# Five of the last fourteen output stores issued from ScalarE's queue instead of SyncE's

## The chip, the core and the metric

The kernel runs on one core of a Trainium2 chip. The metric is the device time of one execution in microseconds (us); of several runs the median is taken. The engines are named as in the profile: PE (TensorE matmuls) and PEld (its weight loads), DVE (VectorE), ACT (ScalarE), POOL (GpSimd) and SP (SyncE). SPq and ACTq are the instruction queues of SP and ACT when they issue a DMA.

## The reference

Two sequence layers over 2048 positions and 640 channels are computed from separate inputs and put side by side in one output of 2048 rows and 1280 columns, in bf16.

```
# part A: a diagonal state-space layer (S5)
Bu = einsum("bld,pd->blp", x, B_bar)
for t in range(L): h = Lam_bar * h + Bu[:, t]          # complex, 640 states
y  = 2 * einsum("blp,dp->bld", hseq, Cmat).real + x * Dskip

# part B: shift filter, gate, long convolution, gate (H3)
kv = shift_filter(k) * v                                # 4 taps
y  = irfft(rfft(kv) * rfft(ssm_k)) + kv * ssm_D         # 4096-point transforms along the sequence
y  = q * y

out = concatenate([a, b], axis=-1)
```

## The kernel before, in words

Everything lives in one large SBUF tile, `arena`, and one PSUM tile, `acc`. Part A computes its recurrence as a tree of matmuls over blocks of 16 rows. Its last stage is `project` (L696 to L719), once for each of the 16 row residues: it loads 128 rows of x (L700), multiplies them by Dskip (L701, on DVE or POOL), runs 20 matmuls into PSUM (L711), adds the two on DVE (L715), and stores 128 rows of 640 columns (L719, 160 KB, rows of 1280 bytes). One residue, the last in time, is cut into two halves of 320 columns, each with its own L715 and L719 of 80 KB. The four x buffers are used in turn, so a load L700 must wait until the store that last read its buffer has landed.

Part B is a convolution by two-step transforms, done in two halves of 320 channels. Its last step, `r1` (L907 to L934), leaves PSUM through a DVE multiplication by q (L932), and `store` (L936 to L944) writes the result. Each call of `store` issues four DMAs of 32 partitions by 16 rows by 160 columns: 160 KB in 512 pieces of 320 bytes. There are 16 of these in all; the last eight, of the second half of the channels, become ready when L932 has run for the last time on their rows.

Nothing is scheduled at run time. Each step is recorded as an operation with a number; the table `ORDER` (L1055) lists all 796 in the order in which they are emitted, each with its engine letter (T for PE, V for DVE, A for ACT, G for POOL, S for SP) and a PSUM bank. So `790S0` is operation 790 on SP. Every engine runs its own list strictly in order: an instruction that waits holds up all that stand behind it on its engine. An operation that needs another's result waits on a semaphore of the engine that made it.

A DMA tells of its end through one of eight semaphores, DMAHW0 to DMAHW7. They are handed out in turn over all the DMAs of SP and ACT together, and a DMA is issued only when the one that held its semaphore before has landed completely. So no more than eight are under way, and a DMA of one queue may have to wait for one of the other.

The operations that matter here are, by number: the part B stores 565 to 568 and 571 and 574 (first half of the channels), 699 to 702 and 709 to 712 (second half); the part A stores 757, 795, 790, 777 and the two half stores 782 and 785; and 773, the last load of x, which feeds 774 (L701 on POOL) and with it the DVE addition 776 whose result 777 stores.

Of the kernel before, what the change touches and what calls it, by code (L numbers as in the profile page):

```python
# [20 lines left out]
PACT, PDVE, PPOOL, PPE, PSP = "A", "V", "G", "T", "S"  # L21
# [443 lines left out]
class PartA:  # L465
# [230 lines left out]
    def project(self, i):  # L696
        c, P, A = self.c, self.c.P, self.A
        rows = lambda t: t.rearrange("(s r) d -> r s d", r=16)[ROW0[i]]
        ys, src = c.v("YS", 640 * (i % 4), 640), rows(self.x2)
        P.add(f"ld_r{i}", {PSP: .5}, lambda e: e.dma_start(out=ys, in_=src), outs=[ys], nbytes=128 * 1280)  # L700
        P.add(f"xd{i}", {PDVE: dve(640, .52), PPOOL: 1.5}, lambda e: e.tensor_tensor(out=ys, in0=ys, in1=c.DR, op=ALU.mult), outs=[ys], ins=[ys, c.DR])  # L701
        lo = (2 if i == 0 else 1) if i < 2 else i % 2
        lh = [A[:, j, i // 2, lo:lo + 255:2] for j in range(10)]
        cuts = ((0, 1), (1, 2)) if i == 13 else ((0, 2),)
        for b0, b1 in cuts:
            g = P.group(b1 - b0)

            def mm(e, B, b0=b0, b1=b1):
                for b in range(b0, b1):
                    for j in range(10):  # L710
                        e.matmul(B[:, 512 * (b - b0):512 * (b - b0) + 320], lhsT=lh[j], rhs=self.CT[:, j, 320 * b:320 * b + 320],  # L711
                                 start=(j == 0), stop=(j == 9))
            ct, part = self.CT[:, :, 320 * b0:320 * b1], ys[:, 320 * b0:320 * b1]
            P.add(f"C{i}", {PPE: (b1 - b0) * 10 * .1355}, mm, ins=lh + [ct], group=g, nmm=10 * (b1 - b0))
            P.add(f"ev_C{i}", {PDVE: dve(320 * (b1 - b0))}, lambda e, B, part=part, n=b1 - b0: e.tensor_tensor(  # L715
                out=part.rearrange("p (b n) -> p b n", b=n), in0=B.rearrange("p (b n) -> p b n", b=n)[:, :, 0:320],
                in1=part.rearrange("p (b n) -> p b n", b=n), op=ALU.add), outs=[part], ins=[part], group=g)
            dst = rows(c.out)[:, 320 * b0:320 * b1]
            P.add(f"st_A{i}", {PSP: .5}, lambda e, dst=dst, part=part: e.dma_start(out=dst, in_=part), ins=[part], nbytes=128 * 640 * (b1 - b0))  # L719


class PartB:
# [213 lines left out]
    def store(self, hf, b0, nb):  # L936
        c, P = self.c, self.c.P
        Q = self.q[hf].rearrange("p (b x) -> p b x", x=160)
        for ce in range(4):
# [1 line left out]
            c0 = 640 + 320 * hf + 160 * el  # L941
            s = Q[32 * ce:32 * ce + 32, b0:b0 + nb, :]
            dst = c.out.rearrange("(a b) d -> a b d", b=64)[:, 32 * cc + b0:32 * cc + b0 + nb, c0:c0 + 160]
            P.add(f"st_B{hf}", {PSP: .2 + .02 * nb}, lambda e, s=s, dst=dst: e.dma_start(out=dst, in_=s), ins=[s], nbytes=32 * nb * 320)  # L944


KSETS = [(0, 1, 2), (3, 4, 5), (6, 7)]
# [88 lines left out]
def plain_order(P):  # L1036
# [17 lines left out]

ORDER = (  # L1055
# [39 lines left out]
)  # L1095


# [68 lines left out]
```

## Time and profile before

| what | value |
|---|---|
| median of 3 runs | 193.33 us (193.14 to 193.49) |
| span of the profiled execution, first to last instruction | 195.7 us |
| PE busy | 181.7 us, 93% |
| DVE, ACT, POOL busy | 165.3, 140.9, 78.1 us |
| queue q1 (SP's DMAs) | 103004 packets, 28.86 MB, 81.1% of 16 engines' span |

The profile shows one execution, and it is 2.4 us longer than the median of the runs without a profile; its own time is known only as its span of 195.7 us. Times below that come with a place ("at 185.08") count from the start of that span. In a timeline row stand the start, the length from there to the end of the last merged instruction, the engine, the line, the operation, what it writes and reads, the count, and in brackets the idle time before it. Rows of a DMA queue give the time for which the sequencer was occupied with issuing, not the transfer. The landing of a transfer is given from the start of its issue.

### The profile page before, as it was taken

How to read it: one execution, taken by the hardware profiler on the slowest of the kernel's cores; microseconds unless marked ns; L12 is line 12 of the kernel's file. 1: busy time of each engine (PE TensorE's matmuls, PEld its weight loads, DVE VectorE, ACT ScalarE, POOL GpSimd, SP SyncE). 2: the span in 40 equal slices, each digit the busy share in tenths (PEclk: the TensorE clock that was granted, in tenths of full speed). 3: DMA queues.
4: the chain of work that ended last, by engine and by line, in shares of the span. 5: the costliest groups of instructions: out<-in, count | busy, mean ns of one | idle time of the engine just before them, and what ended most of it. 6: DMA issues, size and time to landing. Idle time of an engine off the chain costs nothing.

```text
span 195.7 us, 7455 instructions
## 1 busy us (share of the span) xinstructions
PE 181.7 (93%) x3297; PEld 120.1 (61%) x3300; DVE 165.3 (84%) x228; ACT 140.9 (72%) x170; POOL 78.1 (40%) x62
## 2 busy tenths in 40 slices
PE   7699699999999999889998999999999999999980
PEld 2586334444455666565676675557678776977750
DVE  4686999337999898999999999999999999969840
ACT  2499936999999899999988999888747750750000
POOL 8979940530030000196805480876050209302020
PEclk9999979999999999999999999999999999999998
DMA  5999869989699999979993899511199970536985
GB/s 153 259 195 176 135 131 151 185 131 135 129 249 183 243 244 123 156 149 152 126 138 147 208 189 158 106 36 35 35 219 184 189 155 3 134 107 157 211 192 154
DMA packets 103786, 30.15 MB, mean 154 GB/s; under 512 B 97482, under 2 KB 103114, under 8 KB 103754
## 3 DMA queue, kind: packets, MB, share of 16 engines
q1 hardware_dynamic: 103004, 28.86, 81.1%
q10 hardware_dynamic: 750, 0.82, 1.4%
q8 instruction: 26, 0.43, 0.9%
q14 instruction: 6, 0.05, 0.1%
HBM read 12.30 MB, written 7.86 MB: 103 GB/s over the span
## 4 chain that ended last, share of the span: by engine, by line
PE 69%; ACT 10%; DMA 8%; DVE 5%; issue 4%; SPq 2%; ACTq 0%; DVEq 0%
PE acc L711 21%; PE acc L552 19%; PE acc L899 6%; PE acc L854 5%; DMA arena<-in_B_ssm_k_dram 4%; PE acc L571 4%; ACT arena L867 4%; PE acc L835 4%; PE acc L673 3%; PE acc L920 3%; DMA arena<-in_A_B_re_dram 2%; SPq L761 2%; PE acc L830 2%; ACT arena L498 2%; PE acc L672 1%
## 5 line engine op out<-in xcount | busy, mean ns | idle before, releaser
L552 PE MATMUL acc<-arena 128*128 128x512 bf16 (+1 forms) x220 | 47.8, 375 | 1.9 <-DVE arena L402 1.9
L711 PE MATMUL acc<-arena 128*128 128x320 bf16 x320 | 45.7, 299 | 0.0
L867 ACT CAST arena<-acc 128x960 bf16<-128x960 f32 (+1 forms) x40 | 35.2, 907 | 7.0 <-PE acc L854 6.4
L711 PEld LDWEIGHTS <-arena 128*128 128x128 bf16 x320 | 30.4, 98 | 12.6 <-ACT arena L867 0.4
L552 PEld LDWEIGHTS <-arena 128*128 128x128 bf16 x220 | 21.9, 102 | 23.7 <-DVE arena L402 2.2
L840 ACT CAST arena<-acc 128x1024 bf16<-128x1024 f32 x32 | 31.1, 1027 | 2.0 <-PE acc L835 1.5
L904 ACT CAST arena<-acc 128x1024 bf16<-128x1024 f32 x16 | 15.6, 1029 | 10.8 <-PE acc L899 10.8
L854 PE MATMUL acc<-arena 128*64 128x160 bf16 x512 | 22.2, 235 | 0.4 <-ACT arena L867 0.3
L701 POOL TENSOR_TENSOR arena<-arena 128x640 bf16<-128x640 bf16 x8 | 11.7, 1473 | 26.1 <-DMA arena<-in_A_x_dram 26.1
L854 PEld LDWEIGHTS <-arena 128*64 128x64 bf16 x512 | 17.9, 109 | 5.8 <-issue 1.7
L794 POOL TENSOR_TENSOR arena<-arena 128x2048 bf16<-128x2048 bf16 x2 | 8.5, 4246 | 28.3 <-DVE arena L198 28.3
L715 DVE TENSOR_TENSOR arena<-acc,arena 128x640 bf16<-128x640 f32 (+1 forms) x17 | 13.1, 782 | 6.3 <-PE acc L711 6.1
L883 POOL TENSOR_TENSOR arena<-arena 128x1280 bf16<-128x1280 bf16 x4 | 11.3, 2824 | 16.7 <-DVE arena L881 11.0
L794 DVE TENSOR_TENSOR arena<-arena 128x2048 bf16<-128x2048 bf16 x13 | 16.0, 1233 | 1.3 <-ACT arena L199 1.2
L840 DVE CAST arena<-acc 128x1024 bf16<-128x1024 f32 x8 | 9.7, 1221 | 6.8 <-PE acc L835 6.7
L673 PE MATMUL acc<-arena 128*128 128x512 bf16 (+2 forms) x50 | 12.8, 327 | 0.0
L835 PEld LDWEIGHTS <-arena 64*64 64x64 bf16 x960 | 9.3, 107 | 4.9 <-issue 1.3
L881 POOL TENSOR_TENSOR arena<-arena 128x1280 bf16<-128x1280 bf16 x3 | 7.8, 2617 | 11.0 <-ACT arena L867 6.1
L932 DVE TENSOR_TENSOR arena<-acc,arena 128x960 bf16<-128x960 f32 (+1 forms) x12 | 11.9, 1036 | 0.0
L878 DVE TENSOR_TENSOR arena<-arena 128x2560 bf16<-128x2560 bf16 x8 | 11.9, 1483 | 0.0
L835 PE MATMUL acc<-arena 64*64 64x64 bf16 x960 | 11.3, 194 | 0.4 <-ACT arena L840 0.2
L692 DVE TENSOR_TENSOR arena<-acc,arena 128x1024 bf16<-128x1024 f32 (+1 forms) x10 | 11.1, 1137 | 0.5 <-PE acc L673 0.5
(143 smaller groups left out, 309.9 us busy)
## 6 DMA issues: line engine op xcount, KB each, us to landing
out_dram<-arena SPq DMA_DIRECT2D x31, 160.0 KB, 3.2
arena<-in_B_ssm_k_dram SPq DMA_DIRECT2D x8, 320.0 KB, 4.8
kv_rows<-arena SPq DMA_DIRECT2D x5, 512.0 KB, 3.9
arena<-kv_rows SPq DMA_DIRECT2D x16, 160.0 KB, 4.4
arena<-in_A_x_dram SPq DMA_DIRECT2D x16, 160.0 KB, 3.4
arena<-in_B_q_dram SPq DMA_DIRECT2D x8, 320.0 KB, 5.5
arena<-in_A_B_re_dram ACTq DMA_DIRECT2D x3, 160.0 KB, 3.4
arena<-in_A_B_im_dram SPq DMA_DIRECT2D x3, 160.0 KB, 3.5
```

The costliest lines, as they stand in the source:

```text
L552: e.matmul(o, lhsT=self.BT[j][:, d, :], rhs=self.XP[:, d, lo:lo + n], start=(d == 0), stop=(d == 4), skip_group_check=True)
L673: e.matmul(B[:, o], lhsT=c.RR[:, n, j, :], rhs=fr(j, q, k), start=not by_pe, stop=True, skip_group_check=True)
L711: e.matmul(B[:, 512 * (b - b0):512 * (b - b0) + 320], lhsT=lh[j], rhs=self.CT[:, j, 320 * b:320 * b + 320], start=(j == 0), stop=(j == 9))
L715: P.add(f"ev_C{i}", {PDVE: dve(320 * (b1 - b0))}, lambda e, B, part=part, n=b1 - b0: e.tensor_tensor(out=part.rearrange("p (b n) -> p b n" ...
L794: P.add(f"ca{d}_{j}", tt, lambda e: e.tensor_tensor(out=t1, in0=t1, in1=t2, op=ALU.add), outs=[t1], ins=[t1, t2])
L835: e.matmul(B[64 * b:64 * b + 64, 512 * l + 64 * i:512 * l + 64 * i + 64], lhsT=lh[i][ps], rhs=F[ps, b, 64 * l:64 * l + 64], start=True, st ...
L840: P.add(f"e1{what}{hf}_{u}", {PACT: act(1024), PDVE: dve(1024)}, lambda e, B: c.CP[e](out=out, in_=(B.rearrange("p (l n s k) -> p k s l n" ...
L854: e.matmul(B[64 * s:64 * s + 64, 512 * b + 160 * i:512 * b + 160 * i + 160], lhsT=c.W[:, k, 64 * b:64 * b + 64], rhs=self.AS[hf][:, k, 160 ...
L867: c.CP[e](out=out, in_=b.rearrange("p r (k j n) -> p r k j n", k=n, j=4) if nj > 1 else b.rearrange("p r (k x) -> p r k x", k=n))
L878: P.add(f"pp{hf}", n1, lambda e: e.tensor_tensor(out=pt, in0=X, in1=Yk, op=ALU.mult), outs=[pt], ins=[X, Yk])
L904: P.add(f"er2{hf}_{u}", {PACT: act(1024), PDVE: dve(1024)}, lambda e, B: c.CP[e](out=out, in_=B.rearrange("p (s n b) -> p b s n", s=2, n=4 ...
L932: e.tensor_tensor(out=Q, in0=B.rearrange("p (g x) -> p g x", g=2)[:, :, 0:80 * n].rearrange("p g (x n) -> p g x n", n=40), in1=Q, op=ALU.mult)
```

## The change

Five operations get the letter A instead of S in `ORDER`: the part B stores 710, 700 and 699, the part A store 790, and the first of the two half stores, 782. The two calls that record stores allow ACT as an engine. No store changes its size, source or destination, and the list of operations has the same order.

```
-            P.add(f"st_A{i}", {PSP: .5}, lambda e, ...
+            P.add(f"st_A{i}", {PSP: .5, PACT: .5}, lambda e, ...
-            P.add(f"st_B{hf}", {PSP: .2 + .02 * nb}, lambda e, ...
+            P.add(f"st_B{hf}", {PSP: .2 + .02 * nb, PACT: .5}, lambda e, ...
 ORDER, its last rows:
-    574S0 696V6 711S0 779V0 795S0 698V0 788T6 710S0 701S0 774G0 700S0 709S0 780T0 783T1 789V6 776V2 790S0 702S0 699S0 777S0 781V0 784V1 782S0 785S0
+    574S0 696V6 711S0 779V0 795S0 698V0 788T6 710A0 701S0 774G0 700A0 709S0 780T0 783T1 789V6 776V2 790A0 702S0 699A0 777S0 781V0 784V1 782A0 785S0
```

On SP, from load 773 to the end of the program, the queue stood so before (the operations are 773, 574, 711, 795, 710, 701, 700, 709, 790, 702, 699 and 777; the two half stores 782 and 785, which follow, are left out):

```order
L700 DMA arena<-in_A_x_dram 128x640 [waits DMAHW7_49,DMAHW1_49]
L944 DMA out_dram<-arena 32x16x160 [waits DMAHW0_49]
L944 DMA out_dram<-arena 32x16x160
L719 DMA out_dram<-arena 128x640 [waits DMAHW2_49,DVE_49]
L944 DMA out_dram<-arena 32x16x160 [waits DMAHW3_49]
L944 DMA out_dram<-arena 32x16x160 [waits DMAHW4_49,DVE_49]
L944 DMA out_dram<-arena 32x16x160 [waits DMAHW5_49]
L944 DMA out_dram<-arena 32x16x160 [waits DMAHW6_49]
L719 DMA out_dram<-arena 128x640 [waits DMAHW7_49,DVE_49]
L944 DMA out_dram<-arena 32x16x160 [waits DMAHW0_49]
L944 DMA out_dram<-arena 32x16x160 [waits DMAHW1_49]
L719 DMA out_dram<-arena 128x640 [waits DMAHW2_49,DVE_49]
```

All these issues are SP's. The same stretch of SP with the change, from load 773 to the end of the queue (773, 574, 711, 795, 701, 709, 702, 777, 785):

```order
L700 DMA arena<-in_A_x_dram 128x640 [waits DMAHW3_49,DMAHW1_49]
L944 DMA out_dram<-arena 32x16x160 [waits DMAHW4_49]
L944 DMA out_dram<-arena 32x16x160 [waits DMAHW6_49]
L719 DMA out_dram<-arena 128x640 [waits DMAHW7_49,DVE_49]
L944 DMA out_dram<-arena 32x16x160 [waits DMAHW0_49,DVE_49]
L944 DMA out_dram<-arena 32x16x160 [waits DMAHW1_49]
L944 DMA out_dram<-arena 32x16x160 [waits DMAHW2_49]
L719 DMA out_dram<-arena 128x640 [waits DMAHW3_49,DVE_49]
L719 DMA out_dram<-arena 128x320 [waits DMAHW4_49,DVE_49]
```

Five issues have left SP, and the load and the nine stores that stay wait on other DMA semaphores than before. At the end of ACT's queue, behind its last cast L904, now stand 710, 700, 790, 699 and 782:

```order
L904 CAST arena<-acc 128x256x4 [waits DVE_49]
L944 DMA out_dram<-arena 32x16x160 [waits DMAHW3_49,DMAHW5_49,DMAHW0_49,DVE_49]
L944 DMA out_dram<-arena 32x16x160 [waits DMAHW7_49,DVE_49]
L719 DMA out_dram<-arena 128x640 [waits DMAHW1_49,DVE_49]
L944 DMA out_dram<-arena 32x16x160 [waits DMAHW6_49,DMAHW4_49,DMAHW2_49]
L719 DMA out_dram<-arena 128x320 [waits DMAHW5_49,DVE_49]
```

Before, nothing stood behind that cast. Which DMA held a semaphore before follows from the turn in which they are handed out; the framework places the five of ACT earlier in that turn than they stand in `ORDER`. This is the turn of the end of the program, read out of the two built programs:

| | DMAHW0 | 1 | 2 | 3 | 4 | 5 | 6 | 7 |
|---|---|---|---|---|---|---|---|---|
| before, first round | 571 | 757 | 567 | 566 | 568 | 565 | 712 | 773 |
| second | 574 | 711 | 795 | 710 | 701 | 700 | 709 | 790 |
| third | 702 | 699 | 777 | 782 | 785 | | | |
| changed, first round | 571 | 757 | 567 | 710 (ACT) | 566 | 568 | 565 | 700 (ACT) |
| second | 712 | 790 (ACT) | 699 (ACT) | 773 | 574 | 782 (ACT) | 711 | 795 |
| third | 701 | 709 | 702 | 777 | 785 | | | |

A DMA waits for the one above it in its column to land. So with the change 773 waits for 710, 795 for 700, 709 for 790, and 702 for 699: four issues of SP wait for the landing of a store that ACT issues.

More of the change, by code (lines that the diff above doesn't have):

```diff
@@ L718, in project @@
             dst = rows(c.out)[:, 320 * b0:320 * b1]
-            P.add(f"st_A{i}", {PSP: .5}, lambda e, dst=dst, part=part: e.dma_start(out=dst, in_=part), ins=[part], nbytes=128 * 640 * (b1 - b0))
+            P.add(f"st_A{i}", {PSP: .5, PACT: .5}, lambda e, dst=dst, part=part: e.dma_start(out=dst, in_=part), ins=[part], nbytes=128 * 640 * (b1 - b0))
 class PartB:
@@ L943, in store @@
             dst = c.out.rearrange("(a b) d -> a b d", b=64)[:, 32 * cc + b0:32 * cc + b0 + nb, c0:c0 + 160]
-            P.add(f"st_B{hf}", {PSP: .2 + .02 * nb}, lambda e, s=s, dst=dst: e.dma_start(out=dst, in_=s), ins=[s], nbytes=32 * nb * 320)
+            P.add(f"st_B{hf}", {PSP: .2 + .02 * nb, PACT: .5}, lambda e, s=s, dst=dst: e.dma_start(out=dst, in_=s), ins=[s], nbytes=32 * nb * 320)
 KSETS = [(0, 1, 2), (3, 4, 5), (6, 7)]
```

75 rows, old and new, of the table ORDER are left out of this document.

## The prediction

> **What bounds the kernel now.** I read the busy time by stretches of the last 16 us first, then the timeline there, then the chain of waits, then the landing times of stores. The columns of the stretches are: stretch, its length, busy time and count of PE, PEld, DVE, ACT and POOL, granted clock, busy share of the 16 DMA engines, GB/s.
>
> ```profile
> 180.00:183.50 3.50, 3.50 (x145) 2.68 (x144) 3.50 (x5) 0.00 (x0) 0.00 (x0) 1.00 0.99 220
> 183.50:184.00 0.50, 0.50 (x6) 0.36 (x4) 0.50 (x2) 0.00 (x0) 0.00 (x0) 1.00 0.20 42
> 184.50:187.50 3.00, 3.00 (x24) 2.17 (x23) 0.83 (x2) 0.00 (x0) 1.40 (x1) 1.00 0.97 237
> 187.50:188.00 0.50, 0.50 (x5) 0.35 (x4) 0.50 (x2) 0.00 (x0) 0.00 (x0) 1.00 0.43 99
> 188.00:193.50 5.50, 1.93 (x15) 1.18 (x12) 1.70 (x4) 0.00 (x0) 0.00 (x0) 1.00 0.93 220
> 179.70:193.50 13.80, 10.23 (x194) 7.31 (x191) 7.82 (x11) 0.00 (x0) 1.40 (x1) 1.00 0.90 210
> ```
>
> PE sets the pace until 190, at full clock; ACT does nothing here. The DMA engines are nearly full from 180 to 193.5, with two holes, and idle for 0.10 x 13.8 = 1.4 us in all. The timeline of the same stretch:
>
> ```profile
> 173.01 1.93 ACT L904 CAST arena<-acc 128x1024 bf16<-128x1024 f32 x2 [1.16 <-PE acc L899]
> 177.37 3.28 DVE L932 TENSOR_TENSOR arena<-acc,arena 128x960 bf16<-128x960 f32 x3
> 178.54 3.07 SPq L944 DMA_DIRECT2D out_dram<-arena  x5
> 181.71 1.63 SPq L700 DMA_DIRECT2D arena<-in_A_x_dram  x1
> 183.38 0.96 SPq L944 DMA_DIRECT2D out_dram<-arena  x2
> 184.26 0.81 DVE L932 TENSOR_TENSOR arena<-acc,arena 128x640 bf16<-128x640 f32 x1
> 184.44 0.51 SPq L719 DMA_DIRECT2D out_dram<-arena  x1
> 184.99 3.42 SPq L944 DMA_DIRECT2D out_dram<-arena  x4
> 185.85 1.40 POOL L701 TENSOR_TENSOR arena<-arena 128x640 bf16<-128x640 bf16 x1 [8.59 <-DMA arena<-in_A_x_dram]
> 187.25 1.95 DVE L715 TENSOR_TENSOR arena<-acc,arena 128x640 bf16<-128x640 f32 x3 [2.17 <-PE acc L711]
> 188.51 0.87 SPq L719 DMA_DIRECT2D out_dram<-arena  x1
> 189.42 1.36 SPq L944 DMA_DIRECT2D out_dram<-arena  x2
> 189.97 0.49 DVE L715 TENSOR_TENSOR arena<-acc,arena 128x320 bf16<-128x320 f32 x1 [0.76 <-PE acc L711]
> 190.88 1.91 SPq L719 DMA_DIRECT2D out_dram<-arena  x3
> ```
>
> From 178.5 on SP issues with hardly a pause, about 0.61 us apiece (5 in 3.07). The last addition on DVE ends at 189.97 + 0.49 = 190.46, but the store of its result, the last of three in the last row, is issued only at 192.2. It is 1.7 us late because the queue ahead of it is long. What follows on it:
>
> ```profile
> SPq L1161 <- DMA out_dram<-arena: 1.9, 2, 1.7
> L719 SPq DMA_DIRECT2D out_dram<-arena x1: 619/619/619, 192.2 to 192.2; - x1
> 189.97 0.49 DVE arena L715
> ```
>
> The first row (SP's own waits) says that SP, done with issuing at 190.88 + 1.91 = 192.79, waits 1.9 us more for stores: the last lands at 194.7, that is 2.5 us after its issue. Another 1.0 us of closing semaphores makes the span of 195.7. The last row is the last piece of the chain of waits: it ends with DVE at 190.46, since it doesn't follow SP's queue, so the final 5 us have to be read off SP and the DMAs. What can move the end is the moment at which operation 785, the last half store, is issued, and how long it takes to land.
>
> **The change part by part.** What is removed: five issues of about 0.6 us from SP's stretch between 181.7 and 192.8, some 3.0 us. On ACT they cost nothing to compute: its last cast ends at 173.01 + 1.93 = 174.94, so nothing is queued behind the five. The bytes and pieces of the transfers are the same. An issue from ACT costs about the same as from SP:
>
> ```profile
> 2.17 0.45 ACTq L488 DMA_DIRECT2D arena<-in_A_B_im_dram  x1
> ```
>
> What is added are waits of SP for landings of ACT's stores, by the turn of the eight DMA semaphores: 773 for 710, 795 for 700, 709 for 790, 702 for 699. Before, each of SP's DMAs in this stretch waited for one that SP had issued eight places earlier and that had landed already: the chain of waits and SP's waits name no such hold between the stores. Now the partner in each pair is ready late, since it itself waits for DVE. The price of such a wait is the time from issue to landing, minimum/median/maximum: first the part B stores issued at 178.5 to 181.0, then those from 185.0 to 190.2, then part A stores from 184.4 to the end, then the load 773, then the loads of the last 26 us, then all part A stores, and the one part B store at 165.8 that had little beside it.
>
> ```profile
> DMA to landing us min/median/max: 3.1/3.8/4.4
> DMA to landing us min/median/max: 3.2/3.6/4.4
> DMA to landing us min/median/max: 2.9/3.1/3.3
> DMA to landing us min/median/max: 4.0/4.0/4.0
> arena<-in_A_x_dram SPq DMA_DIRECT2D x3, 160.0 KB, 3.1
> DMA to landing us min/median/max: 1.8/2.8/6.2
> DMA to landing us min/median/max: 2.6/2.6/2.6
> ```
>
> Now in order of time.
>
> *710 and 773.* 710 needs the third L932 of its row, which ends at 177.37 + 3.28 = 180.65. ACT issues it then (before: 184.99), and it lands 3.8 us later, at 184.5. SP has sent 712 by 181.6 and stands before load 773 until 184.5; before, it issued it at 181.7. The load lands at 184.5 + 3.1 = 187.6 instead of 181.71 + 4.0 = 185.7. POOL's 1.40 us and about 0.1 us ahead of it follow: 189.1 instead of 187.25. Addition 776 waits for that and ends at 189.1 + 0.83 = 189.9 (DVE L715, 479 to 826 ns, the row below) instead of 188.8; the two half additions follow, 0.48 and 0.49, so the last ends at 190.9 instead of 190.46. Price at the end: nothing as long as 785 is issued after 190.9, which the next steps make sure of; 0.4 us if they don't.
>
> ```profile
> L715 DVE TENSOR_TENSOR arena<-acc,arena x4: 479/653/826, 187.3 to 190.0; 128x640 bf16<-128x640 f32 x2, 128x320 bf16<-128x320 f32 x2
> ```
>
> *700 and 795.* SP sends 574 and 711 from 184.5 to 185.7 and stands before 795. 700 needs the L932 that ends at 184.26 + 0.81 = 185.07; issued then from ACT, it lands 3.6 later, at 188.7. SP sends 795 at 188.7 (before 184.44) and 701 at 189.3, and is free at 189.9.
>
> *790 and 709, 699 and 702.* 790 needs the first L715 of its row, which ends at 187.25 + 0.83 = 188.08. ACT issues 790 at 188.1 and, 0.6 later, 699 at 188.7. The first lands 3.1 later, at 191.2, and lets SP send 709 until 191.8. The second lands 3.6 later, at 192.3, and only then can SP send 702. Behind it stand 777 at 192.9 and 785 at 193.5 (pitch 0.6). 785 lands 2.5 us later, as before: 196.0.
>
> Before, it landed at 194.7. **The sum** is 188.1 + 0.6 + 3.6 + 2 x 0.6 + 2.5 = 196.0, that is 1.3 us more. The closing 1.0 us stays. Against its own time the profiled execution goes from 195.7 to 197.0; I carry the same 1.3 us over to the median of the runs, which lies 2.4 us under that span: 193.3 + 1.3 = 194.6.
>
> Bounds of the sum: with the shortest rows (2.6 for 699, a pitch of 0.48 as in the two issues that took 0.96, 1.8 for 785) the end is 188.1 + 0.5 + 2.6 + 1.0 + 1.8 = 194.0, or 0.7 less than now. With the longest (4.4, a pitch of 0.87, 3.3) it is 188.1 + 0.9 + 4.4 + 1.7 + 3.3 = 198.4, or 3.7 more. I take the medians of the crowded stretch, because what is held back (795 and 701) goes out at 188.7 to 189.9, beside 790 and 699: the four compete for the same 16 engines.
>
> A rule of the Trainium skill speaks against any gain: "DMA: Bandwidth & Descriptors", section "Issuing engines are not separate DMA queues", says that DMAs of different issuers share the same 16 engines and interleave, so that spreading them saves only the sequencer's issue time. The trace agrees as far as it goes, with shares of 0.99, 0.97 and 0.93; by that rule alone the most to be saved is the lag of 1.7 us, of issue time, and the sum would end near nothing. The same page, section "Queues, rings and completion order", says that an increment of a DMA's semaphore lands only after every earlier write of that engine, across its queues; no row here shows that, and it would lengthen the landings on which SP waits, not shorten them.
>
> **The rivals.** *Faster: the relief of SP wins.* If the landings that SP waits for come soon, SP has no backlog and sends 785 as soon as DVE is done: at 190.5 to 190.9, and 2.5 later it has landed, at 193.0 to 193.4, a gain of 1.3 to 1.7. The engines' idle time of 1.4 us caps that; with one half of the holes filled it is 0.7. Time: 192.0 to 192.6. The point from which it decides: 785 must be sent before 192.2, so 702 before 191.0 and 699 must land within 2.3 us of 188.7. For it speaks that SP, not DVE, is late now, and that the DMA engines are emptier while SP stands still; against it, that no part B store in the trace landed in less than 2.6.
>
> *No change: the DMA engines are the bound.* The same bytes must go through engines that are 93% busy to the end. If 699 lands in 3.0, the pitch is 0.5 and 785 lands in 2.3, the end is 188.6 + 3.0 + 1.0 + 2.3 = 194.9: 0.2 us more, time 193.5. For it speaks that a store that is held back finds emptier engines later; against it, that the issue is held in turn, pair by pair, so that emptied engines stay empty.
>
> *Much slower.* A part B store of this stretch took 4.4 us to land. If 699 does that and the rest is as forecast, the end is 0.8 later still, 196.8, a loss of 2.1; time 195.4 and above. For it speak the four stores competing from 188 on; against it, that the 4.4 were seen earlier, with PE still running and more stores under way.
>
> *The five don't come early on ACT.* They would, if the queue of ACT held them up. It is empty of work from 174.94, so I give this nothing.
>
> **How the numbers follow.** A change below 0.2% (0.4 us) can't be told from none. The forecast, a loss of 0.4 to 2.1 us, has 0.54 and its own range of 193.8 to 195.4; much slower has 0.12, no change 0.16, faster 0.18. That makes 0.66 for slower, 0.16 for the same, 0.18 for faster. The predicted time is 194.6. The range that should hold 8 in 10 must take in no change and the edge of the faster case, and most of the heavy one: 192.9 to 195.8.
>
> **What would show it.** In the changed kernel's timeline SP's issue of L700 should stand near 184.5, with a gap of 2 to 3 us ahead of it; the L719 behind the next two L944 near 188.7, with another gap; POOL's L701 should end near 189; SP's last L719 should be issued near 193.5; and SP's waits should name DMA out_dram ahead of L944 and L719, which they don't now. DMA shares should show holes near 183 to 185 and 187 to 189. The prediction is wrong if SP's last L719 is issued before 192, or if L700 goes out at 181.7 as before, which would mean that the DMA semaphores aren't shared between the queues as I read them.

## The result, and the profile after

| | median | ratio to before | 95% interval |
|---|---|---|---|
| before | 193.24 us (192.97 to 193.49) | | |
| with the change | 195.75 us (194.93 to 198.71) | 1.0109 | 1.0070 to 1.0148 |
| the same pair in a later comparison (e7 below) | 195.61 us beside 193.51 | 1.0099 | 1.0064 to 1.0134 |

The change makes the kernel about 1% slower: by the two ratios 2.1 and 1.9 us, where 1.3 us were forecast. The ratio leaves out the longest of the four runs with the change, 198.71 us, and the profile below is of that run, so positions in it are compared with each other, and lengths from PE's last matmul on, not its span with that of before.

From the timeline of the changed kernel, the stretch that was shown of before (up to 180 everything lies 0.44 us earlier here than there):

```profile
176.21 4.01 DVE L932 TENSOR_TENSOR arena<-acc,arena 128x640 bf16<-128x640 f32 x4
180.24 4.78 ACTq L944 DMA_DIRECT2D out_dram<-arena  x2
181.17 8.33 PE L711 MATMUL acc<-arena 128*128 128x320 bf16 x60
185.02 0.36 SPq L700 DMA_DIRECT2D arena<-in_A_x_dram  x1
185.43 1.24 SPq L944 DMA_DIRECT2D out_dram<-arena  x2
187.48 0.74 SPq L719 DMA_DIRECT2D out_dram<-arena  x1
187.68 0.36 ACTq L719 DMA_DIRECT2D out_dram<-arena  x1
188.15 0.38 ACTq L944 DMA_DIRECT2D out_dram<-arena  x1
188.31 4.23 SPq L944 DMA_DIRECT2D out_dram<-arena  x3
189.36 1.39 POOL L701 TENSOR_TENSOR arena<-arena 128x640 bf16<-128x640 bf16 x1 [12.74 <-DMA arena<-in_A_x_dram]
190.79 1.62 DVE L715 TENSOR_TENSOR arena<-acc,arena 128x640 bf16<-128x640 f32 x3 [3.15 <-POOL arena L701]
192.04 0.36 ACTq L719 DMA_DIRECT2D out_dram<-arena  x1
192.64 1.05 SPq L719 DMA_DIRECT2D out_dram<-arena  x2
```

The load 773 (L700) goes out at 185.02, where before it went out at 181.71. Three stores of SP that need no DVE result of that time, 701, 709 and 702, take 4.23 us from the start of the first to the end of the third instead of 0.6 each. POOL's L701 starts at 189.36 instead of 185.85. SP's own waits in this stretch (what waited, for what, us in total, times, longest):

```profile
SPq L700 <- DMA out_dram<-arena: 4.1, 1, 4.1
SPq L944 <- DMA out_dram<-arena: 3.2, 2, 2.3
SPq L1160 <- DMA out_dram<-arena: 2.0, 2, 1.9
SPq L719 <- DMA out_dram<-arena: 0.7, 1, 0.7
```

The row of the closing line existed before (L1161 there). A row of L700 did too, with 1.4 us, but for the load before 773, which went out at 176.15; before, neither 773 nor any store behind it waited for a landing. Now the other three rows are the four new waits for landings: 773 4.1 us, 795 0.7, and the 3.2 us of L944 are 2.3 of 709 (for 790) and 0.9 of 702 (for 699). Together that is 8.0 us in which SP stands still. The chain of waits of the second profile (e7) names the first of them:

```profile
176.79 1.07 DVE arena L932
177.89 4.48 DMA out_dram<-arena
182.43 3.59 DMA arena<-in_A_x_dram
186.13 1.43 POOLq L1160
188.80 0.40 DVE arena L715
```

The L932 that ends at 177.86 releases a store of ACT, whose landing 4.48 us later releases SP's load, whose landing releases POOL (its piece is named by the instruction behind it), and then the last additions. Before, the end of this chain was plain matmul work and one addition. And the DMA engines, in stretches of the changed kernel, columns as before:

```profile
179.30:182.90 3.60, 3.60 (x146) 2.75 (x145) 3.60 (x5) 0.00 (x0) 0.00 (x0) 1.00 1.02 223
182.90:185.50 2.60, 2.60 (x21) 1.87 (x20) 1.75 (x3) 0.00 (x0) 0.00 (x0) 1.00 0.28 61
191.00:192.50 1.50, 0.00 (x0) 0.00 (x0) 1.41 (x3) 0.00 (x0) 0.00 (x0) 1.00 0.49 105
180.00:195.00 15.00, 9.50 (x188) 6.91 (x187) 7.09 (x11) 0.00 (x0) 1.39 (x1) 0.95 0.79 184
```

A share of 0.28 for 2.6 us while 773 is held, and 0.49 for 1.5 us at the end, for most of which 702 is held: holes that later work doesn't fill. From 180 to 195 the share is 0.79; before it was 0.90 from 179.7 to 193.5.

### The profile page after: what moved, and what is told of

Its sections match the earlier page's. It is cut to its first block, busy times and chain, and to the rows that moved or that the text cites. A ratio compares the mean times of both kernels' runs of the same rounds, so it can differ in the third digit from the quotient of the medians.

```text
span 196.8 us, 7460 instructions
## 1 busy us (share of the span) xinstructions
PE 180.6 (92%) x3297; PEld 118.8 (60%) x3300; DVE 165.5 (84%) x228; ACT 141.1 (72%) x170; POOL 78.1 (40%) x62
## 4 chain that ended last, share of the span: by engine, by line
PE 59%; DMA 15%; DVE 8%; issue 6%; SPq 4%; ACT 4%; POOLq 1%; DVEq 1%
PE acc L552 20%; PE acc L711 14%; PE acc L899 6%; DMA arena<-in_B_ssm_k_dram 4%; PE acc L571 4%; PE acc L854 4%; DMA arena<-in_A_B_im_dram 4%; PE acc L835 4%; DMA arena<-kv_rows 3%; PE acc L673 2%; DMA out_dram<-arena 2%; DMA arena<-in_A_x_dram 2%; DVE arena L932 2%; ACT arena L867 2%; SPq L761 2%
## 5 line engine op out<-in xcount | busy, mean ns | idle before, releaser
L711 PE MATMUL acc<-arena 128*128 128x320 bf16 x320 | 45.7, 299 | 0.0
L711 PEld LDWEIGHTS <-arena 128*128 128x128 bf16 x320 | 30.4, 98 | 12.6 <-ACT arena L867 0.4
L701 POOL TENSOR_TENSOR arena<-arena 128x640 bf16<-128x640 bf16 x8 | 11.7, 1475 | 29.7 <-DMA arena<-in_A_x_dram 29.7
L904 ACT CAST arena<-acc 128x1024 bf16<-128x1024 f32 x16 | 15.5, 1027 | 10.8 <-PE acc L899 10.8
L932 DVE TENSOR_TENSOR arena<-acc,arena 128x960 bf16<-128x960 f32 (+1 forms) x12 | 12.0, 1038 | 0.0
```

Of the source, the lines that this page charges most:

```text
L904: P.add(f"er2{hf}_{u}", {PACT: act(1024), PDVE: dve(1024)}, lambda e, B: c.CP[e](out=out, in_=B.rearrange("p (s n b) -> p b s n", s=2, n=4 ...
L932: e.tensor_tensor(out=Q, in0=B.rearrange("p (g x) -> p g x", g=2)[:, :, 0:80 * n].rearrange("p g (x n) -> p g x n", n=40), in1=Q, op=ALU.mult)
```

## The experiments

The theory: SP loses time because its issues wait for landings of ACT's stores, through the semaphores that the two queues share. The rivals: a store issued from ACT, or two queues at once, lands later in itself; or the DMA engines are full and everything else is a detail. All ratios are to the kernel before on the same chip, with 95% intervals. The tail is the length from the end of PE's last matmul to the end of the span in the kernel's profile: its last row of L711 and its span give it. It leaves out what happened earlier in that execution. In the first profile of before the row was

```profile
181.61 8.33 PE L711 MATMUL acc<-arena 128*128 128x320 bf16 x60
```

so PE ended at 189.94, and the tail was 195.7 - 189.94 = 5.8 us.

| run | on ACT | SP's issues held by ACT's stores | ratio | 95% interval | tail, us |
|---|---|---|---|---|---|
| before, e5 | none | none | 1.0004 | 0.9979 to 1.0028 | 5.8, 5.5 |
| the change, e7 | five | four | 1.0099 | 1.0064 to 1.0134 | 7.3, 7.1 |
| e1, e6 | the same five | none | 0.9985; 1.0005 | 0.9940 to 1.0030; 0.9976 to 1.0034 | 4.2, 4.5 |
| e2 | 782 | one | 1.0077 | 1.0046 to 1.0109 | 7.4 |
| e8 | 710 | one, 1.1 us, early | 1.0009 | 0.9974 to 1.0045 | 5.6 |
| e4 | four | three, not the load | 1.0102 | 1.0062 to 1.0142 | 7.1 |
| e3 | seven | none that delays it | 1.0000 | 0.9953 to 1.0046 | 4.9 |
| e9 | none, 3 extra loads | none | 1.0021 | 0.9987 to 1.0055 | 5.6 |
| e10 | the five of e1, 3 extra loads | none (785 1.0 us, by SP's own 702) | 0.9989 | 0.9949 to 1.0029 | 5.3 |

**e1: the same five stores, another turn of semaphores.** The framework interleaves the engines' lists by a model of time before it hands out the semaphores. An option makes it use another model:

```
-    with _tile.TileContext(nc) as tc:
+    with _tile.TileContext(nc, schedule_with_timeline_sim=True) as tc:
```

Every engine's list keeps its order; only the DMA semaphores of the end of the program differ. The kernel before comes out the same with and without it. The turn is now 571, 757, 567, 566, 568, 565, 710, 712, then 773, 574, 711, 795, 700, 701, 709, 702, then 790, 699, 777, 782, 785.

> The change itself, with every engine's list in the same order and the same five stores on ACT; only the turn in which the eight DMA semaphores are handed out is another (the framework interleaves the engines by another model of time). Now 773 waits for 571, 795 for 566, 709 for 710 and 702 for 712, 785 for 700: all of them landed early. Theory of the holds (SP waits for late landings of ACT's stores): no hold is left, SP's load 773 goes out near 181.7 again, the last store is issued within 0.6 us of DVE's end, and the time falls under that of before: 192.3 us (191.8 to 192.9). Rival of the two queues (issuing from ACT or interleaving two queues slows the landings themselves): the loss stays, 195.0 to 196.5 us. Rival of the full DMA engines: no change against before, 193.0 to 193.5.

From its timeline, and SP's waits in it:

```profile
180.87 0.88 SPq L700 DMA_DIRECT2D arena<-in_A_x_dram  x1
188.27 2.00 SPq L719 DMA_DIRECT2D out_dram<-arena  x2
189.41 0.49 DVE L715 TENSOR_TENSOR arena<-acc,arena 128x320 bf16<-128x320 f32 x1 [0.77 <-PE acc L711]
SPq L1160 <- DMA out_dram<-arena: 2.3, 2, 2.1
SPq L719 <- DVE arena L715: 1.9, 2, 1.2
SPq L944 <- DVE arena L932: 1.6, 2, 1.3
```

193.26 us, ratio 0.9985: the whole loss is gone with the waits, though the same five stores come from ACT's queue at the same places. No issue is held by a store's landing any more, SP waits for DVE instead, and its last store goes out with the end of the last addition. So ACT as an issuer costs nothing that the interval shows (0.3% at most, where the change loses 1%), and the rival of the two queues falls. The gain that the theory expected as well, about 1 us, is not there in the times.

**e2: one store on ACT, with one late wait.** Against before, one letter in the order table (with ACT allowed for stores, as in the change), which by the turn makes 702 wait for 782:

```
-782S0
+782A0
```

> One store alone on ACT, 782, the first half store; its place in the turn makes SP's 702 wait for its landing. Theory of the holds: 782 is issued at 189.2 after its DVE addition and lands near 192.1; SP stands before 702 until then, and 702, 699, 777 and 785 follow at 0.5 to 0.6 us, so the last landing is near 196.2 instead of 194.7 and the time is 194.8 us (194.2 to 195.6), although four of the five are back on SP. Rival of the two queues: with one store of 80 KB on ACT a fifth of the loss at most, 193.2 to 193.8. Rival of SP's relief: 192.7 to 193.2.

```profile
184.50 0.80 SPq L719 DMA_DIRECT2D out_dram<-arena  x1
185.63 0.35 ACTq L719 DMA_DIRECT2D out_dram<-arena  x1
188.39 0.85 SPq L944 DMA_DIRECT2D out_dram<-arena  x2
SPq L944 <- DMA out_dram<-arena: 3.1, 1, 3.1
```

195.35 us, ratio 1.0077. SP is done with 790 at 185.30 and sends 702 at 188.39, the moment that 782 has landed; from 186.3 to 188.4 the DMA engines stand at a share of 0.20. One late wait of 3.1 us costs three quarters of the change's loss, with four of the five stores back on SP.

**e8: one store on ACT, without a late wait.** Again one letter, of 710 instead; then 795 waits for it, which was expected to land about when SP gets there.

```
-710S0
+710A0
```

> One store alone on ACT as in e2_one_held, but 710 instead of 782: the one issue of SP that has to wait for it is 795, and 710 has landed near 184.5, when SP gets there anyway. Theory of the holds: no loss, ratio 0.996 to 1.002, against 1.008 for the other single store. Rival that any store on ACT costs: 1.004 to 1.010 as there.

```profile
SPq L719 <- DMA out_dram<-arena: 1.1, 1, 1.1
190.25 1.88 SPq L719 DMA_DIRECT2D out_dram<-arena  x3
```

Ratio 1.0009. The wait is 1.1 us, early in the stretch, and SP has caught up by its last row, so nothing is left of it at the end (the tail is 5.6 us). With e2 this says that it isn't the number of stores on ACT that counts, but which landing SP has to wait for.

**e4: the change without the late load.** Store 710 is on SP, the other four on ACT. 773 waits for 567; the new waits are 795 for 700, 701 for 790, 709 for 699 and 785 for 782.

```
-710A0
+710S0
```

> The change with store 710 back on SP: 773 then waits for 567 and goes out near 181.7, but 795 waits for 700, 701 for 790, 709 for 699 and 785 for 782. Theory of the holds, if the queue's chain of stores alone carries the loss: POOL's L701 ends near 187.3 and DVE near 190.5 as before, SP sends 701 when 790 has landed (near 191), 709 when 699 has (near 192.2), 785 near 194, and the time is 195.0 us (194.3 to 196.0). If the late load carries it: as before or faster, 192.5 to 193.5. Rival of the two queues: about four fifths of the loss, 194.5 to 195.5, but with SP's issues going out on time.

```profile
184.63 1.40 POOL L701 TENSOR_TENSOR arena<-arena 128x640 bf16<-128x640 bf16 x1 [8.45 <-DMA arena<-in_A_x_dram]
188.97 0.49 DVE L715 TENSOR_TENSOR arena<-acc,arena 128x320 bf16<-128x320 f32 x1 [0.76 <-PE acc L711]
191.81 1.28 SPq L719 DMA_DIRECT2D out_dram<-arena  x2
SPq L719 <- DMA out_dram<-arena: 4.0, 1, 4.0
SPq L944 <- DMA out_dram<-arena: 2.3, 3, 1.0
```

Ratio 1.0102, as with the change. Here POOL is on time and DVE ends 0.5 us after PE (180.61 + 8.32 = 188.93), so the load isn't needed for the loss: the queue of stores carries it alone, 6.3 us of SP's waiting in the last two rows. Of these, 4.0 are 795's and 1.0 is that of 709, while 785 was not held, and 1.0 is 711's wait for 565, a store of SP itself. The late load is real, but in the change it runs beside the other chain.

**e3: seven stores on ACT, no late wait of a store.** 574, 711, 795, 710, 709, 701 and 700 are on ACT. SP's waits are 773 for 566, 790 for 795, 777 for 701 and 785 for 700.

> Seven stores on ACT (574, 711, 795, 710, 709, 701, 700) and a turn in which no issue of SP waits for a late one: 773 waits for 566 and 757, 790 for 795, 777 for 701, 785 for 700. Theory of the holds: nobody is held, SP has only 773, 790, 702, 699, 777, 782 and 785 left; faster than before, 192.2 us (191.6 to 192.9). Rival of the two queues: more on ACT is worse than the change, 195 to 197 us. Rival of the full DMA engines: as before, 193.0 to 193.5.

```profile
181.25 5.94 ACTq L944 DMA_DIRECT2D out_dram<-arena  x4
183.20 1.06 SPq L700 DMA_DIRECT2D arena<-in_A_x_dram  x1
188.25 1.39 POOL L701 TENSOR_TENSOR arena<-arena 128x640 bf16<-128x640 bf16 x1 [12.02 <-DMA arena<-in_A_x_dram]
189.68 1.62 DVE L715 TENSOR_TENSOR arena<-acc,arena 128x640 bf16<-128x640 f32 x3 [2.24 <-POOL arena L701]
```

Ratio 1.0000, not the gain that was expected. The load went out at 183.20 and POOL could start only at 188.25: about 4.9 us for a load that took 4.0 before, now beside ACT's early stores. The last addition ended at 189.68 + 1.62 = 191.30 and the last store followed it at 191.45, so in this profile the later load set the end. The tail is shorter than before all the same, which the times don't show.

**e5, e6, e7: before, e1 and the change once more, with new profiles.** They were to say whether e1's shorter tail is real.

> The kernel before, unchanged: for a second profile of it, since the first one is a single execution. Expected of all theories: ratio 1.000; from PE's last matmul to the end of the span 5.8 us as in the first profile (5.3 to 6.3). If it is nearer 4.5, the lag of 1.7 us that SP showed in the first profile is not always there, and the relief of SP is worth less than 1.6 us.

> The change with the other turn of semaphores, as in e1_turn, once more and beside a second profile of the kernel before. Theory of the holds: no loss. What is open is the gain: its tail from PE's last matmul to the end was 4.2 us in the profile against 5.8 before, which would be worth 1.6 us (0.8%), while the times showed 0.15% with an interval of 0.45% to either side. If the tail decides, the ratio is 0.992 to 0.996; if the lag of the first profile was a chance, 0.997 to 1.001.

> The change, unchanged, for a second profile and a better interval. Theory of the holds: ratio 1.007 to 1.013; tail from PE's last matmul to the end 7.3 us (6.8 to 7.8); load 773 is issued the moment 710 has landed, 702 the moment 699 has, and DVE's last addition ends 2 to 3 us after PE's last matmul instead of 0.5.

The last issues of SP in e5, e6 and e7, in this order, each below PE's last row of the same profile:

```profile
179.20 8.32 PE L711 MATMUL acc<-arena 128*128 128x320 bf16 x60
187.91 2.12 SPq L719 DMA_DIRECT2D out_dram<-arena  x3
178.37 8.32 PE L711 MATMUL acc<-arena 128*128 128x320 bf16 x60
185.60 2.00 SPq L719 DMA_DIRECT2D out_dram<-arena  x2
178.82 8.32 PE L711 MATMUL acc<-arena 128*128 128x320 bf16 x60
190.09 1.04 SPq L719 DMA_DIRECT2D out_dram<-arena  x2
```

PE ends at 187.52, 186.69 and 187.14; SP is through with issuing 2.5, 0.9 and 4.0 us after that. The tails repeat the first profiles within 0.4 us. The times repeat too: 1.0099 for the change, 1.0005 for e1's turn. So the profile shows a tail that is 1.0 to 1.6 us shorter without the late waits than before, and the times, some twenty runs of that turn, show no gain. One of the two must have another part in it, and the next pair was made for that. The trace does give a ground for the shorter tail: in the 8 us up to PE's end the DMA engines' share is 1.00 in e1 and 0.89 in e5, so the relieved queue fills holes of nearly a microsecond.

**e9 and e10: how much SP's lag is worth.** Three small loads, of 128 rows of 40 bytes, stand on SP ahead of store 777; nothing else needs them.

```
+    for k in range(3):
+        d, s = c.v("SK", 0, 20) if k == 0 else c.v("PV", 20 * k, 20), a.x2[128 * k:128 * k + 128, 0:20]
+        c.P.add("probe", {PSP: .5}, lambda e, d=d, s=s: e.dma_start(out=d, in_=s), outs=[d], nbytes=128 * 40)
 ORDER:  ... 699S0 796S0 797S0 798S0 777S0 ...
```

> The kernel before with three small extra loads (128 rows of 40 bytes, into places no longer read) on SP just ahead of store 777; nothing waits for them but SP's own queue, and the output is the same. It asks whether SP's lag behind DVE of 1.7 us is there in the timed runs too, since relieving it in e1_turn and e6_turn_again shortened the tail of the profile by 1.3 us and moved the times by nothing. If SP is late in the timed runs as in the profile, three more issues of 0.45 to 0.6 us move the end by their full length: 1.4 to 1.8 us, ratio 1.007 to 1.009. If SP has slack in the timed runs, by less than 0.6 us: ratio under 1.003.

> The same three loads ahead of 777 in the kernel of e1_turn (five stores on ACT, no late hold). In its profile SP stands idle for 1.3 us ahead of the last store, so most of the 1.5 us is absorbed. If SP's relief is real in the timed runs: ratio 0.999 to 1.003, and 0.006 under e9_probe_before. If SP has as much slack in the kernel before: both alike.

For e9, PE's last row, the three extra loads, the last three stores, the landing of the last two stores, and the DMA engines from 2 to 3 us after PE's end; the last row is the same stretch of e5:

```profile
178.16 8.32 PE L711 MATMUL acc<-arena 128*128 128x320 bf16 x60
186.56 2.01 SPq L1035 DMA_DIRECT2D arena<-in_A_x_dram  x3
188.67 1.34 SPq L719 DMA_DIRECT2D out_dram<-arena  x3
DMA to landing us min/median/max: 1.7/1.7/1.7
188.50:189.50 1.00, 0.00 (x0) 0.00 (x0) 0.00 (x0) 0.00 (x0) 0.00 (x0) 1.00 0.26 22
189.50:190.50 1.00, 0.00 (x0) 0.00 (x0) 0.00 (x0) 0.00 (x0) 0.00 (x0) 1.00 0.92 242
```

The loads take 2.0 us of SP, and SP is through 190.01 - 186.48 = 3.5 us after PE, 1.0 more than in e5, since the three stores behind them go out faster. The last store is issued at 189.6, 3.1 us after PE, where it was 2.2 in the first profile of before and 1.9 in e5. But it lands 1.7 us later instead of some 2.5, and the tail is 5.6 as without the loads. The share of 0.26 says why: the transfers ahead are through, and the last stores find the engines nearly empty. So at the end of the queue a microsecond of lateness costs next to nothing in the profile.

The times agree but settle less. The ratio is 1.0021 with an interval up to 1.0055. That excludes the 1.007 to 1.009 that was expected of 1.4 to 1.8 us; but the loads delayed the last store by only about 1 us, which alone would be about 1.005, just inside the interval. The loads also test only the last three stores, not the holes that SP's lag leaves before PE's end. That the DMA engines, nearly full until then, set the end of the kernel before is what remains, and is not shown by itself. e10 (0.9989) has the loads and no loss either, which fits but tells nothing more apart, because the loads also shifted its turn and 785 stood 1.0 us before the landing of 702.

## Why the prediction was right, and where not

**The waits.** The four pairs read out of the turn of the semaphores are the four holds in the trace, and e1 takes the loss away by changing nothing else. This step is shown. Their sizes were less well seen. The prediction's times make 2.9 us for 773, 3.0 for 795, 1.3 for 709 and 0.5 for 702, 7.7 in all; measured were 4.1, 0.7, 2.3 and 0.9, 8.0 in all. That the totals nearly agree is luck. Store 700 landed after 2.7 us instead of 3.6, and SP got to 795 later than forecast, also because the prediction leaves no time for the issue of 773 itself. Of the holes forecast in the DMA shares, near 183 to 185 and 187 to 189, the first came and the second did not (0.94 from 187 to 189); it came at 191 to 192.5.

**The sum.** In the profile after, everything up to 180 lies 0.44 us earlier than in that of before (the third L932 ends at 176.21 + 4.01 = 180.22 instead of 180.65). With that taken off, the forecast put the issue of 790 at 187.7, of 699 at 188.3, of 702 at 191.9, of 785 at 193.1 and the last landing at 195.6. Measured: 187.68, 188.15, 192.2 (the third of the row 188.31 4.23, less its 0.3), 193.2 (the second of the last row), and 192.64 + 1.05 + 2.0 = 195.7. The landing of 699 took about 4.1 us instead of 3.6, the pitch was 0.5 instead of 0.6. The tail grew by 1.5 and 1.6 us in the two pairs of profiles (7.3 - 5.8 and 7.1 - 5.5), against 1.3 forecast. The 2.4 us between span and median, which the prediction takes over, compare two measures. In each run that has both, the device time is 1.7 to 1.9 us above the span (194.75 and 193.0 in e5), so by estimate the profiled execution of before took some 197.5 us; the 1.3 us carried over do not depend on it.

**The size in the times.** The timed loss is some 2.0 us by the two ratios, about half a microsecond more than the tail shows. The profiles don't say where that is; e1 and e6 are off by about 1.2 us in the same direction (a shorter tail, no gain in time), e2 is not off. It stays open. The median of 195.75 lies inside the range by only 0.05 us, which is partly luck, and 0.35 above the forecast's own range of 193.8 to 195.4, though the loss by the ratios, 2.1 and 1.9, does not exceed its 0.4 to 2.1.

**The late load, costed at nothing.** The price at the end was right: e4 has no late load and the same loss. Its size was too small: 710 took 4.7 us to land (4.5 in e7) instead of 3.8, the load 4.2 instead of 3.1, so POOL was through at 190.75 instead of 188.7 and the last addition ended at 190.79 + 1.62 = 192.41, 2.9 us after PE. It was to be covered by 2.6 us until 785's issue; 0.8 was left. A little more and the load, not the queue, would have set the end.

**What bounds the kernel before.** Here a step failed: "What can move the end is the moment at which operation 785, the last half store, is issued, and how long it takes to land." The two were summed as if they were independent. e9 moved the issue about 1 us back and the landing came as much sooner after it; e1 moved it forward by about 1.6 us and the times show no gain, though the profile's end came sooner. The sum held for the change because the last landing (2.6 us) was as slow there as before (2.5). A likely reason is that the stores behind the last hold go out in a burst, 702, 777 and 785 within a microsecond; that is not shown.

**The rivals.** *Faster* fails at the point that was named: 699 would have had to land in 2.3 us, and took 4.1. Even without any late wait the times show nothing of the relief (e1, e6, e3). *No change, the DMA engines being full*, is wrong for the change and, by the times, right for what it takes away. The Trainium skill, "DMA: Bandwidth & Descriptors", section "Issuing engines are not separate DMA queues", says that several issuers save only the sequencer's issue time. e1 and e6 agree, with ratios of 0.9985 and 1.0005; the change shows that it can also cost, through the waits. *Much slower* put the time at 195.4 and above, and the median of 195.75 is there; its mechanism was half met: 699, the landing that it hung on, took 4.1 us, between the 3.6 of the forecast and its 4.4.

## What to carry to other kernels

Moving a DMA to another queue also moves it in the turn of the completion semaphores, and through them one queue can be made to wait for the landing of the other's transfer; read from the built program, for each DMA, which transfer held its semaphore before, and ask when that one is ready. A store that waits for a late result is a bad predecessor for anything that could go out earlier. And before relieving a queue that seems late, delay it on purpose: if the end doesn't move, the queue wasn't what it waited for at that place.

## What was not expected of the hardware

The time from issue to landing gave way to the issue: the last store lands some 2.5 us after its issue in the kernel before and 1.7 in e9, where it is issued about 1 us later after PE's end, with the end in place. A load of 160 KB took 3.6 to 5.1 us to land when stores from the other queue were under way (3.6 in e7, 4.2 with the change, 4.6 in e1, 5.1 in e8), against the 3.1 at which it was costed; with SP's own stores alone it took 4.0.
